# One attention and mixture-of-experts kernel: the dense layers moved between attention steps, blocks fetched by plain transfers, masks in sixteen TensorE tiles

## The chip, the cores and the metric

The kernel runs on one core of one Trainium2 chip. The metric is the device time of one execution in microseconds (us): the median of the runs, beside the lowest and the highest of them. Every count of instructions and every duration below comes from one profiled execution, whose span reaches from the first to the last instruction. PE is TensorE; its loads of the stationary operand are shown on a line of their own.

## The reference, cut to what matters

The first half is attention with a sliding window of 128 keys and a linear distance bias, for 8 batches, 8 heads, 576 positions and head size 64. The second half takes the result as 4608 tokens of 512 numbers. It adds a dense two-layer network to the output of one of eight experts, which is chosen for each token by the largest of eight logits.

```python
scores = np.where(mask, scale * q @ k.T + bias, -1e9)   # 0 <= i - j < 128
attn = softmax(scores)
x = (attn @ v).transpose(0, 2, 1, 3).reshape(4608, 512)
y_dense = np.maximum(x @ w1_dense, 0.0) @ w2_dense
expert_idx = np.argmax(x @ w_gate, axis=1)
# for the tokens of expert e, with the gate probability as a factor:
y_moe[mask] = gate_w[mask, None] * (np.maximum(x[mask] @ w1[e], 0.0) @ w2[e])
return y_dense + y_moe
```

## The kernel before

**Attention.** A *unit* is one batch and four heads, so there are 16 units. A unit has three *steps*: key tiles 0 and 1, tiles 2 and 3, and the half tile 4 (`KP`, L332). That makes 48 steps (`NS`), numbered n. In each step `scores` (L334) lets PE write the masks and biases of four heads into PSUM by matmuls with an identity (L352), adds q.k in 32-row tiles of the array (L363), and ScalarE takes the exponential (L373). VectorE then splits the result into a high and a low bf16 part (`lo`, L392). One step later `attend` (L395) multiplies with v on PE (L426). Two steps later `norm` (L435) divides on VectorE and writes the f32 token row `xrow` (L442). Three steps later `flip` (L451) turns the row by PE and copies it to `xT` on ScalarE (L470). Between these, VectorE turns keys and queries (`turn`, L158) and splits v (`prep_v`, L177), and ScalarE rounds keys (L171) and queries (L168) for PE.

**Order.** PE, ScalarE and VectorE run in the order in which the program is written down, under `tc.manual_schedule` (L594). The order on GpSimd and SyncE is left to the planner. The score tiles and the `ax` tile of the attend matmuls have one PSUM buffer each; everything else in this stage shares the two buffers of `psum_m`.

**Gate and scatter.** After the last step of a batch, `gate_a` to `gate_d` run one step apart. They compute the logits, the chosen expert, its probability and the place (`slot`) of each token in a region of DRAM that belongs to its expert (`xs_dram`). Then GpSimd scatters the rows, 5 indirect transfers a batch (L569). A row is 516 words: 512 numbers, the gate and the token's number. The expert and dense weights, 18 transfers of 512 KB in bf16, are asked for by GpSimd in every second step from n=6 on, each held back by a small copy that waits for a norm (`tick`, L582). Keys, queries and v are loaded by SyncE, one unit ahead.

**Blocks.** After attention, VectorE computes a table of 43 blocks of 128 tokens, each of one expert (L672 to L749). GpSimd gathers a block's rows indirectly (`fetch`, L764) into one of 5 buffers, 4 blocks ahead. `turn_x` casts to bf16 on VectorE (L777), turns by PE and copies out (L784). `layer1` runs the expert's and the dense first layer (L814, L822) with their relus on ScalarE (L830, L831). `turn_h` turns both (L791), VectorE copies out (L797), and `layer2` sums both second layers in PSUM (L849, L857). VectorE copies the sum (L865) and GpSimd scatters it to the output (L866). In the loop the order is

```python
turn_h(j); layer1(j + 1); turn_x(j + 2); layer2(j); fetch(j + AHEAD)
```

## Time and profile before

| what | value |
|---|---|
| median of 3 runs | 508.16 us (503.89 to 510.34) |
| the profiled execution's own time | 514.72 us |
| its span | 513.0 us |
| PE busy | 383.8 us, 75% of the span |
| VectorE busy | 304.0 us, 59% |
| ScalarE busy | 200.3 us, 39% |
| GpSimd busy | 172.5 us, 34% |
| moved by DMA | 66.92 MB, mean 130 GB/s |
| mean granted TensorE clock | 0.882 |

In the profile's slices each digit is the busy share of one fortieth of the span, 12.8 us, in tenths. A row of the groups gives the line, the engine, the operation, the tiles it writes and reads, their shapes and the count; then busy time and the mean duration of one in ns; then the idle time just before and what ended it. A row of the waits names the instruction that waited and the one that released it, and gives the total in us, the number of times, and the longest. The chain goes back from the last instruction to whatever released each one.

### The profile page before, as it was taken

Reading aid. Unit: us, or ns where it says so; the run is one execution under the profiler, and the core shown is the slowest. Engines: PE = TensorE matmul, PEld = TensorE weight load, DVE = VectorE, ACT = ScalarE, POOL = GpSimd, SP = SyncE. Lnnn points to the kernel's source line nnn. Section 1 sums busy time; section 2 is a strip of 40 time slices with the busy share of each in tenths; the row PEclk is TensorE's granted clock in tenths of the full one; section 3 lists DMA queues with packets and bytes.
Section 4 is the critical chain, followed back from the end, with each engine's and each line's share of the span. In section 5 each row is a group of like instructions: output and inputs, shape, how many; then the busy total and the mean of one; then the engine's idle time right before and its main releaser. Section 6 shows DMA issues by size and latency. Waiting matters only on the chain.

```text
span 513.0 us, 10730 instructions
## 1 busy us (share of the span) xinstructions
PE 383.8 (75%) x4143; PEld 240.0 (47%) x4180; DVE 304.0 (59%) x567; ACT 200.3 (39%) x287; POOL 172.5 (34%) x244
## 2 busy tenths in 40 slices
PE   1567877778776787777783039899998999889891
PEld 0345555555554556555562015444454444445450
DVE  5879797775977669867471514444444444444441
ACT  2527656626567156671541003323333222322230
POOL 2000016042151321613113433445545455535531
PEclk9999878876799768997696559999999999999997
DMA  4644979879698697986102220323323333323210
GB/s 135 178 115 118 201 156 246 186 187 210 153 251 175 186 209 166 255 159 202 45 24 90 74 82 33 115 91 98 102 86 111 101 124 103 114 83 119 80 52 0
DMA packets 70912, 66.92 MB, mean 130 GB/s; under 512 B 42446, under 2 KB 61902, under 8 KB 70864
## 3 DMA queue, kind: packets, MB, share of 16 engines
q0 software_dynamic: 19328, 37.91, 29.5%
q1 hardware_dynamic: 51140, 28.01, 20.1%
q8 instruction: 34, 0.56, 0.4%
q10 hardware_dynamic: 396, 0.33, 0.2%
q14 instruction: 14, 0.11, 0.1%
HBM read 58.56 MB, written 20.78 MB: 155 GB/s over the span
## 4 chain that ended last, share of the span: by engine, by line
PE 24%; DMA 13%; DVE 5%; issue 3%; ACT 3%; POOL 1%; another core or an unknown queue 1%; POOLq 0%; DVEq 0%
DMA xr<-xs_dram,row_i 13%; PE y L849 4%; PE y L857 4%; PE hd L822 4%; PE hm L814 4%; ACT hr L831 2%; PE hps L791 2%; DVE xm L777 2%; PE xps L780 2%; PE ax L426 1%; PE lp L486 1%; POOL xs_dram L569 1%; PE lg L498 1%; DMA xs_dram<-xrow,slot 1%
## 5 line engine op out<-in xcount | busy, mean ns | idle before, releaser
L426 PE MATMUL ax<-vf,p 128*128 128x65 bf16 (+1 forms) x576 | 74.9, 215 | 50.6 <-DVE xrow L442 44.5
L373 ACT ACTIVATE p<-sq 128x1024 f32<-128x1024 f32 (+1 forms) x96 | 69.3, 776 | 92.5 <-PE sq L363 70.8
L392 DVE TENSOR_TENSOR plo<-p 128x1024 bf16<-128x1024 f32 (+1 forms) x96 | 82.6, 900 | 28.6 <-ACT p L373 23.1
L426 PEld LDWEIGHTS <-p 128*128 128x128 bf16 (+1 forms) x1152 | 69.9, 113 | 61.2 <-DVE xrow L442 51.2
L830 ACT ACTIVATE hr<-hm,xr 128x512 bf16<-128x512 f32 x43 | 29.5, 687 | 159.7 <-PE hm L814 159.7
L426 PE MATMUL ax<-vf,plo 128*128 128x65 bf16 (+1 forms) x576 | 74.3, 212 | 3.9 <-DVE plo L392 2.8
L866 POOL DMA_INDIRECT out_dram<-yo,tok_i x43 | 44.5, 1034 | 97.1 <-DVE hT L797 88.5
L426 PE MATMUL ax<-vl,p 128*128 128x64 bf16 (+1 forms) x576 | 74.4, 211 | 0.3 <-issue 0.3
L569 POOL DMA_INDIRECT xs_dram<-xrow,slot x40 | 42.7, 1067 | 87.2 <-DVE xrow L561 44.9
L426 PEld LDWEIGHTS <-plo 128*128 128x128 bf16 (+1 forms) x576 | 63.1, 113 | 3.4 <-DVE plo L392 3.3
L865 DVE COPY yo<-y 128x512 f32<-128x512 f32 x43 | 29.7, 692 | 58.0 <-PE y L857 54.1
L352 PE MATMUL sq<-mask,ident_b 128*128 128x512 bf16 (+1 forms) x177 | 46.9, 370 | 15.0 <-DVE mask L235 9.2
L766 POOL DMA_INDIRECT xr<-xs_dram,row_i x43 | 43.8, 1019 | 19.9 <-ACT hr L831 11.3
L822 PE MATMUL hd<-w_all,xT 128*128 128x512 bf16 x172 | 45.0, 385 | 0.0
L849 PE MATMUL y<-w_all,hT 128*128 128x512 bf16 x172 | 44.2, 379 | 0.9 <-DVE hT L797 0.9
L780 PE MATMUL xps<-ident_b,xm 128*128 128x128 bf16 x172 | 17.3, 225 | 36.4 <-DVE xm L777 35.8
L857 PE MATMUL y<-w_all,hT 128*128 x172 | 44.1, 379 | 0.0
L814 PE MATMUL hm<-w_all,xT 128*128 x150 | 40.7, 388 | 3.8 <-DMA xr<-xs_dram,row_i 2.7
L363 PE MATMUL sq<-qT,kT 32*128 32x256 f32 (+2 forms) x640 | 34.7, 330 | 3.4 <-ACT qT L168 3.4
L588 POOL CAST w_all<-xrow 64x1 bf16<-64x1 f32 x18 | 8.1, 447 | 85.4 <-DVE xrow L442 85.1
L784 DVE COPY xT<-xps 128x512 bf16<-128x512 bf16 x43 | 18.3, 425 | 31.0 <-PE xps L780 31.0
L363 PEld LDWEIGHTS sq<-qT,kT 32*128 32x128 f32 x640 | 26.3, 217 | 21.9 <-issue 14.4
(115 smaller groups left out, 570.2 us busy)
## 6 DMA issues: line engine op xcount, KB each, us to landing
kraw<-in_k_dram SPq DMA_DIRECT2D x16, 576.0 KB
vf<-in_v_dram SPq DMA_DIRECT2D x64, 128.0 KB
w_all<-in_moe_w_dram POOLq DMA_DIRECT2D x16, 512.0 KB
qraw<-in_q_dram SPq DMA_DIRECT2D x62, 128.0 KB
vf<-in_v_dram SPq DMA_DIRECT2D x16, 64.0 KB
w_all<-in_moe_w_dense_dram POOLq DMA_DIRECT2D x2, 512.0 KB
qraw<-in_q_dram SPq DMA_DIRECT2D x15, 64.0 KB
xr<-xs_dram,row_i POOLq DMA_INDIRECT x43, 3.4
```

What stands on the lines that cost most here:

```text
L352: nc.tensor.matmul(out=sq[g // 2][:, g % 2, 0:tot], lhsT=ident_b, rhs=rhs, start=True, stop=False,)
L363: nc.tensor.matmul(out=sq[g // 2][:, g % 2, i * wid : i * wid + nq], lhsT=kT[32 * g : 32 * g + 32, c, kj * P : kj * P + P], rhs=qT[32 * g ...
L373: nc.scalar.activation(out=p32[:, :, 0:tot], in_=sq[i][:, :, 0:tot], func=ACT.Exp, scale=SCALE,)
L392: nc.vector.tensor_tensor(out=plo[:, :, 0:tot], in0=p32[:, :, 0:tot], in1=phi[:, :, 0:tot], op=ALU.subtract,)
L426: nc.tensor.matmul(out=ax[:rows, i, o0 : o0 + w], lhsT=lhs, rhs=rhs, start=(n == 1), stop=(n == 3 * len(kl)),)
L569: ins = nc.gpsimd.indirect_dma_start(out=xs_dram[:, :], out_offset=bass.IndirectOffsetOnAxis(ap=slot[:rows, t : t + 1], axis=0), in_=xrow. ...
L766: nc.gpsimd.indirect_dma_start(out=xm_i.bitcast(I32)[:, :], out_offset=None, in_=xs_dram[:, :], in_offset=bass.IndirectOffsetOnAxis(ap=row ...
L814: nc.tensor.matmul(out=hm, lhsT=xT[:, kc, :], rhs=w_all[:, bass.DynSlice(er, 1), 0, kc, :], start=(kc == 0), stop=(kc == 3),)
L822: nc.tensor.matmul(out=hd, lhsT=xT[:, kc, :], rhs=w_all[:, E, 0, kc, :], start=(kc == 0), stop=(kc == 3),)
L849: nc.tensor.matmul(out=y, lhsT=hT[:, c, :], rhs=w_all[:, E, 1, c, :], start=(c == 0), stop=False,)
L857: nc.tensor.matmul(out=y, lhsT=hT[:, 4 + c, :], rhs=w_all[:, bass.DynSlice(er, 1), 1, c, :], start=False, stop=(c == 3),)
L866: nc.gpsimd.indirect_dma_start(out=out[:, :], out_offset=bass.IndirectOffsetOnAxis(ap=tok_i[:, 0:1], axis=0), in_=yo[:, :], in_offset=None ...
```

## The change

- **Dense layers.** They leave the blocks. `dense1` and `dense2` run between the attention steps of the batches, spread over six steps. The first layer holds weights still and moves tokens, and its relu runs on ScalarE. The second layer's result is copied by ScalarE and scattered by GpSimd into a second table, `ys_dram`, with the slots of the tokens.
- **Rounding.** `norm` writes an f32 tile `xf`. ScalarE rounds it to bf16 into `xrow`, whose rows are now 260 words, and `flip` makes two copies, one f32 for the gate and one bf16 for the dense layer.
- **Gate.** `gate_a` runs per unit instead of per batch, and VectorE adds the two parts up (`gate_av`).
- **Routing.** Sixteen blocks are formed from the first six batches in `route_early`, while attention is still running. The other 27 are formed at the end in `late_table`. Every expert's region ends in 128 rows of filling (`late_fill`), so that a block is always 128 rows in a run.
- **Blocks.** They hold the expert's layers alone. A block's x and y rows come by two plain transfers on SyncE at a register's address, seven blocks ahead of the loop's next one, into ten buffers. ScalarE copies the turned h, and VectorE adds the dense result. One block is written down per pass of the same loop from n=50 on, so the last batch's gates and dense layers lie between the first blocks.
- **Masks.** The mask of each head is stored turned by 32 rows per head. Sixteen 32x32 tiles of the array write it instead of four full matmuls per step; each tile has rows and columns of its own.
- **Loads and memory.** v is asked for two units ahead and has three buffers; its first load waits for the first queries. Several buffers shrink. The order on SyncE is now written by hand during attention. The weights are asked for one per 2.33 steps, from n=4 on.

```diff
     NB = NTOK // P + E - 1
-    NSLOT = (E - 1) * NTOK + NB * P
-
-    RW = DM + 4
-    GC = DM
-    TC = DM + 1
+    NQ = 6
+    NE = 16
+    assert (NQ * S - E * (P - 1) + P - 1) // P >= NE
+    NL = NB - NE
+
+    ST = NTOK + P
+    NSLOT = E * ST
+
+    XW = DM // 2
+    RW = XW + 4
+    GC = XW
+    TC = XW + 1
...
@@ -67,8 +75,10 @@
...
+    ys_dram = dram.tile([NSLOT, DM], I32, name="ys_dram")
     w_all = persist.tile([P, E + 1, 2, 4, FF], BF16, name="w_all")
...
+        g = h % 4
+        n = (P, 32, 64, 32)[g]
+        for r in range(0, P, n):
+            t = (r + 32 * g) % P
+            nc.vector.scalar_tensor_tensor(
+                out=mask[t : t + n, h, :],
+                in0=d_f[r : r + n, :],
+                scalar=-slope / SCALE,
+                in1=big[r : r + n, :],
+                op0=ALU.mult,
+                op1=ALU.add,
+            )
...
+    def mask_rest():
         for h in range(4, H):
             mask_head(h)
...
@@ -341,20 +377,24 @@
...
-        for g in range(4):
+
+        for rot, g in [(i, j) for i in range(4) for j in range(4)]:
             h = 4 * hq + g
+            k0 = 32 * rot
+            r0 = (k0 + 32 * g) % P
             if pr == 0:
-                rhs = mask[:, h, 0:PW].unsqueeze(1).to_broadcast([P, 2, PW])
+                rhs = mask[r0 : r0 + 32, h, 0:PW].unsqueeze(1).to_broadcast([32, 2, PW])
             elif pr == 1:
-                rhs = mask[:, h, 0 : 2 * PW]
+                rhs = mask[r0 : r0 + 32, h, 0 : 2 * PW]
             else:
-                rhs = mask[:, h, 2 * PW - TAIL : 2 * PW]
+                rhs = mask[r0 : r0 + 32, h, 2 * PW - TAIL : 2 * PW]
             nc.tensor.matmul(
-                out=sq[g // 2][:, g % 2, 0:tot],
-                lhsT=ident_b,
+                out=sq[g // 2][k0 : k0 + 32, g % 2, 0:tot],
+                lhsT=ident_b[r0 : r0 + 32, r0 : r0 + 32],
                 rhs=rhs,
                 start=True,
                 stop=False,
+                skip_group_check=True,
             )
...
@@ -435,16 +476,21 @@
         def norm():
             if hq == 0 and pr == 0:
                 cur[("xrow", b)] = xrows[b % 2]
-            xrow = cur[("xrow", b)]
+            xrow = cur[("xrow", b)].bitcast(BF16)
+            xf = xpool.tile([P, 2, 256], F32, name="xf", tag="xf")
...
-            xo = xrow[:rows, qis[0] : qis[0] + nt, hq * 256 : hq * 256 + 256]
             nc.vector.tensor_tensor(
-                out=xo.rearrange("p t (h d) -> p t h d", h=4),
+                out=xf[:rows, 0:nt].rearrange("p t (h d) -> p t h d", h=4),
                 in0=ax_v[:rows, 0:nt, :, 0:D],
                 in1=recip[:rows, 0:nt].unsqueeze(3).to_broadcast([rows, nt, 4, D]),
                 op=ALU.mult,
             )
+            nc.scalar.copy(
+                out=xrow[:rows, qis[0] : qis[0] + nt, hq * 256 : hq * 256 + 256],
+                in_=xf[:rows, 0:nt],
+            )
+            cur[("xf", u, pr)] = cur["xf"] = xf
...
@@ -454,54 +500,70 @@
...
         if hq == 0 and pr == 0:
-            cur[("xT", b)] = xpool.tile([P, 4, S], F32, name="xT", tag="xT", bufs=1)
-        xT = cur[("xT", b)]
-        xrow = cur[("xrow", b)]
+            cur[("xTb", b)] = xpool.tile([P, 4, S], BF16, name="xTb", tag="xTb")
+        if pr == 0:
+            cur["xT"] = xpool.tile([P, 2, S], F32, name="xT", tag="xT", bufs=1)
+        xf = cur.pop(("xf", u, pr))
...
+        for dst in (cur["xT"], cur[("xTb", b)][:, 2 * hq : 2 * hq + 2, :]):
+            nc.scalar.copy(
+                out=dst[:, :, q0 : q0 + nt * rows].rearrange(
+                    "p c (t x) -> p t c x", t=nt
+                ),
+                in_=tp[:, 0:nt, :, 0:rows],
+            )
...
-    def gate_a(b):
-        xT = cur[("xT", b)]
-        HF = S // 2
-        for hf in range(2):
-            lp = psum_m.tile([P, 512], F32, name="lp", tag="misc")
-            for ds in range(4):
+    def gate_a(u):
+        lp = psum_m.tile([P, 512], F32, name="lp", tag="misc")
+        for h, (t0, t1) in enumerate(DT):
+            c0, c1 = t0 * P, min(t1 * P, S)
+            for c in range(2):
+                r0 = 64 * h + 32 * c
                 nc.tensor.matmul(
-                    out=lp[32 * ds : 32 * ds + 32, 0:HF],
-                    lhsT=wg_pad[:, ds, :],
-                    rhs=xT[:, ds, hf * HF : (hf + 1) * HF],
+                    out=lp[r0 : r0 + 32, 0 : c1 - c0],
+                    lhsT=wg_pad[:, 2 * (u % HQ) + c, :],
+                    rhs=cur["xT"][:, c, c0:c1],
                     start=True,
                     stop=True,
                 )
...
+    def gate_av(u):
+        lp = gst["lp"]
+        for p0, w in ((64, LW), (0, DT[0][1] * P)):
+            dst = lt[p0 : p0 + 64, 0:w]
+            if u % HQ == 0:
+                nc.vector.tensor_copy(out=dst, in_=lp[p0 : p0 + 64, 0:w])
+            else:
+                nc.vector.tensor_tensor(
+                    out=dst, in0=dst, in1=lp[p0 : p0 + 64, 0:w], op=ALU.add
+                )
...
@@ -572,61 +634,433 @@
                 in_=xrow.bitcast(I32)[:rows, t, :],
                 in_offset=None,
             )
+            apart("x", b, ins)
+        slots[b] = slot
...
+    def after(nm, ins, nb):
+
+        for b, name in writers[nm]:
+            if b < nb:
+                tc.add_manual_dep(
+                    ins.ins,
+                    name,
+                    mybir.DependencyInfo(
+                        mybir.DependencyClass.Sync, mybir.DependencyReason.DATA
+                    ),
+                    reason="rows written",
+                )
...
+    def dense1(b, c, hf):
...
+        hp = psum_m.tile([P, 512], F32, name="hp", tag="misc")
+        for kc in range(4):
+            nc.tensor.matmul(
+                out=hp[:, 0:HF],
+                lhsT=w_all[:, E, 0, kc, c * P : c * P + P],
+                rhs=xTb[:, kc, c0:c1],
+                start=(kc == 0),
+                stop=(kc == 3),
+            )
+        nc.scalar.activation(out=hT[:, c, 0:HF], in_=hp[:, 0:HF], func=ACT.Relu)
+
+    def dense2(b, t):
...
+        yp = psum_m.tile([P, 512], F32, name="yp", tag="misc")
+        for c in range(4):
+            nc.tensor.matmul(
+                out=yp[:rows, :],
+                lhsT=hT[:, c, t0 * P : t0 * P + rows],
+                rhs=w_all[:, E, 1, c, :],
+                start=(c == 0),
+                stop=(c == 3),
+            )
+        yt = xpool.tile([P, DM], F32, name="yt", tag="yt", bufs=4)
+        nc.scalar.copy(out=yt[:rows, :], in_=yp[:rows, :])
+        ins = nc.gpsimd.indirect_dma_start(
+            out=ys_dram[:, :],
+            out_offset=bass.IndirectOffsetOnAxis(
+                ap=slots[b][:rows, t : t + 1], axis=0
+            ),
+            in_=yt.bitcast(I32)[:rows, :],
+            in_offset=None,
+        )
+        apart("y", b, ins)
+
+    def dense_items(b):
+        one = [lambda c=c, h=h: dense1(b, c, h) for h in range(2) for c in range(4)]
+        two = [lambda t=t: dense2(b, t) for t in range(NT)]
+        return [one[0:2], one[2:4], two[0:2], one[4:6], one[6:8], two[2:5]]
...
+    def route_early():
+        fb = whole(0, "a")
+        zero = rt.tile([1, E], F32, name="zero")
+        nc.vector.memset(zero, 0.0)
+        yield
+        er, ro = yield from table(fb, zero, NE, "a")
...
+        for j in range(NE):
+            where[j] = (er[0:1, j : j + 1], st_i[0:1, j : j + 1])
...
+    def late_counts():
+        base_r = rt.tile([1, E], I32, name="base_r")
+        nc.vector.tensor_copy(out=base_r, in_=basee[0:1, :])
+        nb = whole(P - 1, "b")
...
+    def late_table():
+        nb, eb = where["nb"], where["eb"]
+        er, ro = yield from table(nb, eb, NL, "b")
+
+        nc.vector.tensor_tensor(
...
+    def late_fill():
+        base_r = where["base"]
+        for e in range(E):
+            r = nc.values_load(
...
+            ins = nc.sync.dma_start(
+                out=xs_dram[bass.DynSlice(r, P), :], in_=fill_x.bitcast(I32)[:, :]
+            )
+            apart("x", NQ, ins)
+            ins = nc.sync.dma_start(
+                out=ys_dram[bass.DynSlice(r, P), :].rearrange("p (a f) -> p a f", a=2),
+                in_=fill_x.bitcast(I32)[:, 0:XW].unsqueeze(1).to_broadcast([P, 2, XW]),
+            )
+            apart("y", NQ, ins)
...
+    def fetch(j):
+        r = nc.values_load(
...
+        xr = mpool.tile([P, RW], F32, name="xr", tag="xr", bufs=10)
+        yr = mpool.tile([P, DM], F32, name="yr", tag="yr", bufs=10)
+        for nm, t, src in (("x", xr, xs_dram), ("y", yr, ys_dram)):
+            ins = nc.sync.dma_start(
+                out=t.bitcast(I32)[:, :], in_=src[bass.DynSlice(r, P), :]
+            )
+            if j < NE:
+                tc.declare_no_dep(
+                    ins.ins, group=nm + "late", reason="rows of the first NQ batches"
+                )
+                tc.add_to_no_dep_group(nm + "late", ins.ins)
+            after(nm, ins, NQ if j < NE else B)
+        st[("r", j)] = (xr, yr)
...
+    def turn_x(j):
+        xr, _ = st[("r", j)]
+        xps = psum_t.tile([P, 4, P], BF16, name="xps", tag="xps")
+        for kc in range(4):
+            nc.tensor.transpose(
+                out=xps[:, kc, :],
+                in_=xr.bitcast(BF16)[:, kc * P : (kc + 1) * P],
+                identity=ident_b,
+            )
+        xT = mpool.tile([P, 4, P], BF16, name="xTm", tag="xTm")
+        nc.vector.tensor_copy(out=xT, in_=xps)
...
+        hp = psum_h.tile([P, FF], F32, name="hpm", tag="hpm")
+        for kc in range(4):
+            nc.tensor.matmul(
+                out=hp,
+                lhsT=xT[:, kc, :],
+                rhs=w_all[:, bass.DynSlice(er, 1), 0, kc, :],
+                start=(kc == 0),
+                stop=(kc == 3),
+            )
+        hr = mpool.tile([P, FF], BF16, name="hr", tag="hr")
+        nc.scalar.activation(out=hr, in_=hp, func=ACT.Relu, scale=xr[:, GC : GC + 1])
...
+    def turn_h(j):
+        hr, er = st.pop(("g", j))
+        hps = psum_t.tile([P, 4, P], BF16, name="hps", tag="xps")
+        for c in range(4):
+            nc.tensor.transpose(
+                out=hps[:, c, :], in_=hr[:, c * P : (c + 1) * P], identity=ident_b
+            )
+        hT = mpool.tile([P, 4, P], BF16, name="hTm", tag="hTm")
+        nc.scalar.copy(out=hT, in_=hps)
...
+    def layer2(j):
+        hT, er = st.pop(("h", j))
+        xr, yr = st.pop(("r", j))
+        y = psum_y.tile([P, DM], F32, name="y", tag="y")
+        for c in range(4):
+            nc.tensor.matmul(
+                out=y,
+                lhsT=hT[:, c, :],
+                rhs=w_all[:, bass.DynSlice(er, 1), 1, c, :],
+                start=(c == 0),
+                stop=(c == 3),
+            )
+        yo = mpool.tile([P, DM], F32, name="yo", tag="yo", bufs=4)
+        nc.vector.tensor_tensor(out=yo, in0=y, in1=yr, op=ALU.add)
...
+    AHEAD = 7
...
+    def block(j):
+        if j == 0:
+            turn_x(0)
+            layer1(0)
+            turn_x(1)
+        turn_h(j)
+        if j + 1 < NB:
+            layer1(j + 1)
+        if j + 2 < NB:
+            turn_x(j + 2)
+        layer2(j)
+        if j + AHEAD + 1 < NB:
+            fetch(j + AHEAD + 1)
...
     with tc.manual_schedule(engines={ENG.PE, ENG.Activation, ENG.DVE}):
+        mask_consts()
         turn(0, "k")
         round_qk(0, "k")
-        mask_consts()
+        mask_head(0)
+        mask_head(1)
         turn(0, "q")
         round_qk(0, "q")
+        mask_head(2)
+        mask_head(3)
...
+        loads = ExitStack()
+        loads.enter_context(tc.manual_schedule(engines={ENG.SP}))
+        while jm < NB:
+            if n == NS:
+                loads.close()
+            if n > NS + 1:
+                block(jm)
+                jm += 1
+            if 0 <= n - 3 < NS:
+                flip(*steps[n - 3])
+                u2, pr2 = steps[n - 3]
+                b2 = u2 // HQ
+                if pr2 == 2:
+                    items.setdefault(n, []).append(lambda u=u2: gate_a(u))
+                    gates.setdefault(n + 1, []).append(lambda u=u2: gate_av(u))
+                if u2 % HQ == HQ - 1 and pr2 == 2:
...
+                    for i, fs in enumerate(dense_items(b2)):
+                        items.setdefault(n + 2 + i, []).extend(fs)
+                    if b2 == NQ - 1:
+                        gen = route_early()
...
+            for f in gates.pop(n, []):
+                f()
             if n == 0:
-                more_constants()
                 prep_v(0)
+            todo = items.pop(n, [])
+            for f in todo[:1]:
+                f()
             if 0 <= n - 1 < NS:
                 norms[n - 1] = attend(*steps[n - 1])
+            for f in todo[1:]:
+                f()
...
                 else:
+                    if u + 2 < NU:
+                        load_v(u + 2)
```

## The prediction

> **What bounds the kernel now.** I read three views in this order: the page's slices, to find the stages; the sums by stretch, to see how full each engine is in each; then the waits and the chain in order of time, to see which wait ends last.
>
> ```profile
> PE   1567877778776787777783039899998999889891
> ...
> DVE  5879797775977669867471514444444444444441
> ACT  2527656626567156671541003323333222322230
> ...
> PEclk9999878876799768997696559999999999999997
> DMA  4644979879698697986102220323323333323210
> ```
>
> Three stages show. Up to slice 22 (some 277 us) is attention: PE and VectorE share the load, ScalarE is half idle, DMA is nearly full. Slices 23 and 24 are a hole. The rest is 43 blocks, with PE alone busy.
>
> ```profile
> 200.00:225.00 25.00, 20.63 (x314) 14.95 (x316) 20.86 (x39) 14.58 (x23) 9.49 (x10) 0.86 0.90 209
> ...
> 275.00:300.00 25.00, 1.95 (x14) 1.74 (x13) 9.19 (x37) 0.24 (x1) 10.00 (x13) 0.50 0.18 60
> ...
> 400.00:450.00 50.00, 46.73 (x305) 24.04 (x310) 24.13 (x46) 14.12 (x22) 24.73 (x33) 1.00 0.35 111
> ```
>
> The columns are PE, weight loads, VectorE, ScalarE, GpSimd, granted clock, DMA share, GB/s. In attention no engine is full (PE and VectorE 21 of 25 us). The waits say why:
>
> ```profile
> ACT p L373 <- PE sq L363: 70.8, 30, 7.7
> ...
> PE ax L426 <- DVE xrow L442: 44.5, 26, 5.5
> ...
> DVE plo L392 <- ACT p L373: 23.1, 12, 4.3
> ```
>
> Exp waits for scores, the attend matmuls (L426) for VectorE's norm, VectorE's split (L392) for exp: a ring of three engines. Unit 4's key transpose (late in step n=9) starts at 60.1 us and the last mask matmuls (n=47) at 259.4: about 5.3 us a step. The hole is the last batch's gates, scatters, routing table and first gather: PE's last gate matmul ends at 276.6, the first block matmul starts at 304.1. The blocks:
>
> ```profile
> 406.81 0.86 PE y L849 x4
> 407.67 0.86 PE y L857 x4
> 408.98 0.86 PE hm L814 x4
> 409.84 0.88 PE hd L822 x4
> 410.74 0.61 ACT hr L831
> 411.38 3.27 DMA xr<-xs_dram,row_i
> ```
>
> From 304 to 503 us is 43 x 4.63 us. A gather can start only when a row buffer is free (after L831), and its 3.3 us end on the path every other block; PE's own work is about 4.2 us of the 4.63.
>
> **The blocks afterwards.** The dense half goes, and so do the x casts, as rows arrive as bf16. PE per block: 4+4 transposes (x8 take 0.45 in the chain) and two groups of four matmuls (0.86 each): 0.45 + 1.72 = 2.17 us. Beside it ScalarE has a relu (0.69, L830) and the copy of the turned h, priced by L831 (0.60): 1.29. VectorE has xT (0.43, L784) and an add, priced by L442's same shape (0.69): 1.12. GpSimd has one scatter of 1.03. The relu has 1.09 us of PE work as cover (4 transposes and layer 2 of the block before), so neither evacuation ends on the path. DMA: x 128 x 1040 B, y 128 x 2048 B, out 128 x 2048 B, 657 KB; at the 400:450 rate (111 GB/s at share 0.35, 317 GB/s full) 2.07 us. Gathers leave GpSimd for SP, issued eight blocks, some 18 us, before use, so the 3.3 us are covered; two direct issues and a register load per block on SP are bounded below by 0.7 (0.34 is the row of a lone key load) and above by 2 us (each queued behind others, as in attention, 1 us): under the block either way. So PE at 2.17, DMA close behind. I take 2.33, PE at its 400:450 share of 0.935: 43 x 2.33 = 100 us, where it was 199. Ends 2.17 (93 us) and 2.9 (126, DMA at attention's rate, 207 GB/s at 0.92).
>
> **The hole.** Blocks 0 to 15 use only batches 0 to 5 and a table made in steps 42 to 46; so block 0 waits for one fetch after attention frees its memory, 3 us (a gather takes 3.3). Batch 7's gates and dense part now sit between blocks 0 and 7: PE 8.1 dense + 2.5 gates = 11 us. VectorE's late gates and table (some 37 small operations of 0.2, L509's row) lie in blocks 2 to 6, beside matmuls; I count 3 of their 7 us. GpSimd has 10 + 8 scatters of 1.05 = 19 us in these 8 steps of about 3.5 us, so they fit, and fetch 16, queued on SP behind the fills and behind every batch-7 scatter, has 7 blocks of cover. If that cover fails, all later fetches stand behind it: up to 10 us.
>
> **Attention afterwards.** Per batch (6 steps):
> - *PE.* Before, 198 us in 275, 24.8 a batch at the granted clock of about 0.85; some 22.6 from warm rows. Dense: layer 1 streams 16 x 256 + 16 x 320 columns, 3.9 us at L849's warm rate (0.86 per 4 x 512); layer 2, 20 matmuls, 4.3. Masks save about 0.8. That is 5.4 us a step at the old clock, 5.0 warm.
> - *ScalarE.* Rows:
>
> ```profile
> L373 ACT ACTIVATE p<-sq 128x1024 f32<-128x1024 f32 x64 | 62.1, 1021 | 89.9 <-PE sq L363 68.2 <-remote 14.2 <-issue 7.5
> ...
> L831 ACT ACTIVATE hr<-hd 128x512 bf16<-128x512 f32 x43 | 25.7, 597 | 6.3 <-PE hd L822 1.2
> ...
> L470 ACT COPY xT<-tp 128x512 f32<-128x512 f32 x32 | 19.0, 593 | 6.2 <-remote 3.2 <-PE tp L464 3.0
> ```
>
>   Before: 145 us, 18.1 a batch. Added: the second flip copy and the rounding of xf, each 4 x 0.59 + 2 x 0.29 = 2.9; eight relus at 0.40 (the 288-wide copy L493); five copies of y at 0.60; gone: two L493. 2.9 + 2.9 + 3.2 + 3.0 - 0.8 = 11.2. 29.3 a batch, 4.9 a step; it was 3.0.
> - *VectorE.* 3.9 a step, plus two adds or copies per unit, 0.8: 4.2. The early table, 5 us once, goes into its gaps.
> - *DMA.* Before, about 13.3 us per engine and unit. ys adds 288 rows per unit, xs rows halve: +1.8 - 0.7, 14.4 in a longer unit, so share 0.8, not above today's. v is asked for two units ahead, which removes most of VectorE's 24 us of DMA waits, some 0.3 us a step. GpSimd gains 40 scatters, 42 us over 240, off the path. Weights come one per 2.33 steps instead of 2, the last at step 44, before any block needs it.
>
> So three engines need 4.2, 4.9 and 5.0 to 5.4 us. The ring, over two steps: split 2.3, norm 0.9, attend 1.5, dense items 1.3, flip 0.6, scores 1.1, first exp 1.0, some 0.6 between engines: 9.3; then ScalarE's key rounding (2.2, L171) ahead of the next flip copies and exp, of which PE work covers half: about 11.5. I take 5.9 a step. Ends: 5.2 (ScalarE nearly gapless) and 6.9 (5.4 at today's PE share, 0.78). 40 steps (10 to 49): 236 us.
>
> *A rule against this.* The Trainium skill, "TensorEngine Tiling (Array Packing)", PSUM Bottleneck, says tiling speeds TensorE but not PSUM evacuation, and wants ScalarE and VectorE both used; here every new evacuation is ScalarE's. By the rows that is 6.2 us of the 11.2 a batch; were it split evenly, ScalarE would need 4.4, VectorE 4.7, and by the rule I would say 5.5 a step, 16 us less. The change doesn't split, so the rows stand.
>
> *Masks.* Four full matmuls take 0.95 us to the first q.k matmul (129.69 to 130.64). The same page (Key Properties) says a tiling-mode switch drains the array, and the change adds one per step; "TensorE: Matmul & The Clock Gate", Measured speedup, gives 660 ns for a 16-tile, 512-column pack. By the pages: 0.95 - 0.66 - a drain. The trace has a drain: 0.42 us of idle weight load before L363, of which 0.21 is the last mask streaming, so 0.2; gain 0.1. By rows: L363's 16 tiles start within 0.35 us, so 0.35 + 0.21 + 0.2 = 0.76, gain 0.2. In 16 narrow steps the sixteen starts cost 0.15 more than today. I take 0.2 x 32 - 0.15 x 16 = 4 us of PE work over all, the drain included (ends -5 and +10); as PE has gaps, 0 on the end.
>
> **Start.** Pieces for three quarters of the heads make 22 mask instructions of 0.62 instead of 8: 14 more, 9 us of VectorE. Six of them sit before the first scores, where q, no longer sharing with v (held behind it by a GpSimd copy), should come earlier. I count +5 (ends 1 and 9): n=10, at about 61 before, starts at 66.
>
> **Sum, on the profiled execution** (span 513.0, own time 514.7): 66 + 236 + 3 + 11 + 3 + 100 = 419; then the tail (503.0 to 513.0, unchanged) 10 and 1.7 around the span: 431. That execution is 1.3% above the median shown (508.16), so against the median 431 x 508.16/514.72 = 425 us.
>
> **Rivals.**
> - *ScalarE and PE overlap almost fully*, 5.2 a step: 28 less, 398. For: no DMA waits. Against: two bufs of psum_m tie PE's items to ScalarE's order. 0.16.
> - *DMA bounds the blocks* at 2.9 us: 26 more, 450. For: 1040-byte rows, two tables, the fills. Against: rows of 2 KB kept 317 GB/s. 0.14.
> - *Early fetches aren't early* (the first blocks wait for the last batch after all): the hole of 28 us returns, 452. 0.06.
> - *The clock drops*, on the other side. PE needs 5.0 us warm per step; at 5.9 a step a granted clock under 0.85 makes PE the ring, and at 0.62 (8.1 us) the result is 2% slower. At 0.58: 8.6 us, 40 x 2.7 = 108 more, 532. For: 0.67 at 100:125 and 0.63 at 242:253. Against: those dips follow idle PE (17.1 of 25 and 7.0 of 11 us busy); dense matmuls fill it. 0.05; near no change 0.05.
> - Main case: 0.54, alone 408 to 446.
>
> Range: lower end short of the first rival, 396; the upper takes in DMA and 6.7 us steps, 468. A measurement of this kernel tells 2% from no change; faster by more 0.90, within 0.05, slower 0.05.
>
> **What would show it.** Right: step spacing of the exps near 5.9 with ScalarE above 80% in attention; no hole; y groups 2.2 to 2.5 us apart at clock 1.0 and DMA share above 0.8. Wrong: steps at 5.2 or 7; a gap before block 16; DMA landing just ahead of the transposes of x; PE's clock under 0.8.

## The result, and the profile after

The changed kernel takes 421.51 us (median of 4 runs, 417.0 to 426.11), the kernel before 509.25 in the same comparison: a ratio of 0.824 (95% interval 0.815 to 0.833). The prediction was 425. The profiled execution took 424.43 us with a span of 422.7; it and one other ran slower than the rest, at a lower mean clock (0.926 and 0.938 against 0.941 to 0.971), and the ratio leaves these two out. One thing has to be known for all that follows: the changed kernel took 419 to 422 us in two of the comparisons (one on chip 1, the other's chip isn't known) and 465 to 466 in two others (chips 15 and 10), while the kernel before stayed between 504 and 516 in all four. No chip is known to have been used in two comparisons, so what belongs to the chip and what to the hour can't be told apart. So kernels are compared only within one group of runs on one chip; each group has its own execution of the changed kernel.

The slices of the changed kernel, now 10.6 us each (busy tenths, granted clock, DMA share):

```profile
PE   1445989499899797898797989887789899999990
...
DVE  7899898679879778889786799861336344444440
ACT  3244785679789787799786799854436555555550
...
PEclk9986586789999998999997999998989999999997
DMA  4454677597979786979886955629938999888720
```

The hole is gone: PE has no slice below 7 from the ninth to the last but one. ScalarE, which showed 1 to 7 in attention before, now shows mostly 7 to 9 beside PE and VectorE. DMA is close to full in attention and again in the blocks. The last attention step's exps lie in slice 27.

The blocks, first by windows (busy PE, weight loads, VectorE, ScalarE, GpSimd, then clock, DMA share, GB/s), then by the chain in order of time (start, length, what):

```profile
350.00:375.00 25.00, 24.36 (x167) 13.30 (x170) 11.85 (x21) 13.32 (x21) 10.01 (x11) 1.00 0.87 278
375.00:400.00 25.00, 24.42 (x170) 13.42 (x172) 11.67 (x22) 13.42 (x21) 10.64 (x11) 1.00 0.86 273
```

```profile
347.78 0.22 PE hps L940 x4
348.00 0.04 issue
348.03 1.02 PE hpm L925 x4
349.06 0.22 PE xps L904 x4
349.28 0.86 PE y L952 x4
```

PE holds 97% of each window. One turn of the chain is 0.22 + 0.04 + 1.02 + 0.22 + 0.86 = 2.36 us, and it contains nothing but PE. The one step that isn't as predicted is `hpm` (the expert's first layer): 1.02 instead of 0.86.

In attention (70 to 280 us) the waits name a different last arrival than before, and so does the chain:

```profile
DVE qs L162 <- DMA qraw<-in_q_dram: 12.5, 6, 4.0
...
DVE plo L433 <- ACT p L414: 6.5, 12, 1.1
```

```profile
190.13 1.39 DVE qs L162
...
193.32 1.10 SPq L140
194.47 12.26 DMA qraw<-in_q_dram
206.92 1.39 DVE qs L162
208.32 0.56 SPq L140
208.93 0.54 SPq L140
209.52 0.53 SPq L140
210.09 0.53 SPq L140
210.66 12.43 DMA qraw<-in_q_dram
```

VectorE's split waits 6.5 us for exp, where it waited 23.1. What the chain runs through is the queries: four issues on SP once the single raw buffer is free, 12 us of transfer, the transpose that frees the buffer, and again. From one transpose at 190.13 to the next at 206.92 it is 16.8 us, and a unit of three steps at 5.48 us takes 16.4.

### The profile page after: what moved, and what is told of

It is laid out like the page before. It is cut to its first block, busy times and chain, and to the rows that moved or that the text cites. A ratio compares the mean times of both kernels' runs of the same rounds, so it can differ in the third digit from the quotient of the medians.

```text
span 422.7 us, 12201 instructions
## 1 busy us (share of the span) xinstructions
PE 345.6 (82%) x4628; PEld 220.3 (52%) x4656; DVE 288.9 (68%) x566; ACT 276.5 (65%) x471; POOL 167.8 (40%) x197
## 4 chain that ended last, share of the span: by engine, by line
PE 25%; DMA 22%; DVE 20%; issue 11%; ACT 6%; POOL 6%; SPq 5%; another core or an unknown queue 1%; POOLq 1%; ACTq 0%; DVEq 0%
DMA qraw<-in_q_dram 18%; DVE plo L433 6%; POOL out_dram L961 6%; PE ax L467 5%; SPq L140 4%; DVE qs L162 4%; PE hpm L925 4%; PE yp L692 3%; PE y L952 3%; PE hp L677 3%; DMA vf<-in_v_dram 2%; DVE xf L483 2%; DVE mask L258 2%; ACT p L414 2%; PE lg L557 1%
## 5 line engine op out<-in xcount | busy, mean ns | idle before, releaser
L467 PE MATMUL ax<-vf,p 128*128 128x65 bf16 (+1 forms) x576 | 70.0, 209 | 19.2 <-DVE xf L483 18.9
L467 PEld LDWEIGHTS <-p 128*128 128x128 bf16 (+1 forms) x1152 | 67.1, 110 | 30.6 <-DVE xf L483 23.9
L961 POOL DMA_INDIRECT out_dram<-yo,xr x43 | 42.6, 991 | 69.0 <-DVE yo L960 46.5
L467 PE MATMUL ax<-vl,p 128*128 128x64 bf16 (+1 forms) x576 | 69.5, 206 | 0.0
L467 PE MATMUL ax<-vf,plo 128*128 128x65 bf16 (+1 forms) x576 | 69.4, 207 | 0.0
L701 POOL DMA_INDIRECT ys_dram<-yt,slot x40 | 47.1, 1178 | 37.4 <-ACT yt L700 27.1
L467 PEld LDWEIGHTS <-plo 128*128 128x128 bf16 (+1 forms) x576 | 60.8, 109 | 0.0
L677 PE MATMUL hp<-xTb,w_all 128*128 128x256 bf16 (+1 forms) x256 | 43.4, 295 | 13.8 <-ACT hTd L684 7.0
L925 PE MATMUL hpm<-w_all,xTm 128*128 x163 | 44.3, 387 | 5.2 <-issue 2.5
L933 ACT ACTIVATE hr<-hpm,xr 128x512 bf16<-128x512 f32 x43 | 29.6, 687 | 23.4 <-PE hpm L925 18.2
L952 PE MATMUL y<-w_all,hTm 128*128 x166 | 43.7, 383 | 1.1 <-ACT hTm L944 0.8
L960 DVE TENSOR_TENSOR yo<-y,yr 128x512 f32<-128x512 f32 x43 | 29.7, 691 | 21.3 <-PE y L952 20.6
L684 ACT ACTIVATE hTd<-hp 128x256 bf16<-128x256 f32 (+1 forms) x64 | 25.6, 411 | 27.1 <-PE hp L677 26.7
L692 PE MATMUL yp<-w_all,hTd 128*128 128x512 bf16 (+1 forms) x147 | 40.1, 381 | 3.8 <-ACT yt L700 1.7
L172 ACT CAST kT<-ks 128x1152 fp32r<-128x1152 f32 x16 | 35.3, 2209 | 2.3 <-DVE ks L162 2.3
L517 ACT COPY xT<-tp 128x512 f32<-128x512 f32 (+1 forms) x48 | 23.1, 481 | 19.9 <-PE tp L510 19.8
```

Source lines behind the costliest of these rows:

```text
L172: nc.scalar.copy(out=d[:, :, 0:S].rearrange("p c (x r) -> p c x r", r=R), in_=s.rearrange("p c (r x) -> p c x r", r=R),)
L467: nc.tensor.matmul(out=ax[:rows, i, o0 : o0 + w], lhsT=lhs, rhs=rhs, start=(n == 1), stop=(n == 3 * len(kl)),)
L677: nc.tensor.matmul(out=hp[:, 0:HF], lhsT=w_all[:, E, 0, kc, c * P : c * P + P], rhs=xTb[:, kc, c0:c1], start=(kc == 0), stop=(kc == 3),)
L692: nc.tensor.matmul(out=yp[:rows, :], lhsT=hT[:, c, t0 * P : t0 * P + rows], rhs=w_all[:, E, 1, c, :], start=(c == 0), stop=(c == 3),)
L701: ins = nc.gpsimd.indirect_dma_start(out=ys_dram[:, :], out_offset=bass.IndirectOffsetOnAxis(ap=slots[b][:rows, t : t + 1], axis=0), in_=y ...
L925: nc.tensor.matmul(out=hp, lhsT=xT[:, kc, :], rhs=w_all[:, bass.DynSlice(er, 1), 0, kc, :], start=(kc == 0), stop=(kc == 3),)
```

## The experiments

Two measures are used beside the medians, both from the traces: a *step* is the mean distance of the first exps from n=10 to n=47, and a *block* the mean distance of the `yo` additions from block 11 to 42. The first four runs shared a chip (15), the next four another (1), the last four a third (10). `before` is the kernel before in the same group.

### First group

`again`: the changed kernel unchanged.

> The changed kernel once more, beside the three kernels of this call, as their base. Expected as before: about 421 us, 0.82 of the kernel before, steps 10 to 47 at 5.5 us each, a unit of three steps every 16.4 us.

Measured 465.28 us (459.24 to 469.61; before 516.01; ratio 0.904, 0.891 to 0.916). Step 6.19 instead of 5.48, block 2.47 instead of 2.36. The instructions on every engine have the same order as in the first trace, so this is no other schedule; more on it under the third group.

`masks_full`: the sixteen tiles undone.

```diff
-        n = (P, 32, 64, 32)[g]
+        n = P
...
-            t = (r + 32 * g) % P
+            t = r
...
-        for rot, g in [(i, j) for i in range(4) for j in range(4)]:
+        for g in range(4):
...
```

> The masks part alone is undone: four full matmuls with the identity per step, and one mask instruction per head. By the prediction's sum the sixteen tiles save 4 us of PE work in all and nothing on the end, and the pieces of the masks cost 9 us of VectorE at the start, of which 5 end on the path: so undoing it makes the kernel 3 to 7 us faster (n=10 near 66 instead of 72 us) with the steps unchanged at 5.5. Rival, PE's order sets the steps: each wide step grows by the 0.4 us that the mask group takes longer (0.65 against 1.04 us), 32 x 0.4 = 13 us, less the 6 won at the start: 7 us slower. Rival, transfers set the steps: steps unchanged, 5 us faster.

Measured 453.39 us (448.16 to 460.1; ratio 0.887, 0.879 to 0.895), 11.9 less than `again`. The first exp of n=10 comes at 66.6 us instead of 71.0, which is the start as predicted: VectorE's mask instructions take 5.4 us in all instead of 15.0, and the very first exp comes at 16.6 instead of 18.8. A step took 6.00 instead of 6.19, another 7 us over 37 steps. The mask matmuls themselves did what they should in the changed kernel: 24.4 us of PE in all, against 41.8 with full masks (groups of `again3` and `masks_full2`, the same two kernels in the third group of runs):

```profile
L391 PE MATMUL sq<-mask,ident_b 32*32 32x512 bf16 (+1 forms) x768 | 24.4, 364 | 15.4 <-DVE mask L258 13.3 <-ACT p L414 1.7
```

```profile
L389 PE MATMUL sq<-mask,ident_b 128*128 128x512 bf16 (+1 forms) x192 | 41.8, 337 | 14.2 <-DVE mask L258 12.5 <-ACT p L412 1.6
```

So the tiles make PE less busy, and yet the kernel with them is the slower one. It would be wrong to read from this that the masks are off the path. A *wide* step is one with two key tiles, two of the three in a unit. In a wide step the first q.k matmul follows the first mask matmul by 0.37 us with tiles and by 0.96 with full masks (medians), and where nothing else is late the distance of two exps that ends with a wide step grows with it, from 3.78 to 4.25 us and from 4.68 to 5.18. What is shorter with full masks is the start, and those steps in which the engines are held; the third group shows them.

`yt_vector`: the copy of the dense result out of PSUM moved from ScalarE to VectorE.

```diff
-        nc.scalar.copy(out=yt[:rows, :], in_=yp[:rows, :])
+        nc.vector.tensor_copy(out=yt[:rows, :], in_=yp[:rows, :])
```

> Only the copy of the dense result out of PSUM (L700, 40 times 0.6 us) moves from ScalarE to VectorE: the evacuations are split between the two engines, as the skill's rule wants. If ScalarE's load sets the steps (the prediction's reading), ScalarE goes from 4.9 to 4.4 us a step and the kernel becomes up to 16 us faster. If the round trip of the queries or the transfers set the steps, the result is within 3 us of the changed kernel. If VectorE's place in the ring counts (split, norm, attend), it is 5 to 15 us slower.

Measured 507.47 us (504.57 to 510.75; ratio 0.991, 0.986 to 0.996): 42 us more than `again`, a step of 7.44. Forty copies of 0.6 us are 24 us of work, so more than the copies is lost. It is the third expected reading, at three times its size. The waits of this kernel between 100 and 300 us:

```profile
DVE yt L700 <- PE yp L692: 31.5, 22, 3.2
PEld L591 <- issue: 17.2, 5, 3.5
...
PE pc L591 <- DVE oh L579: 16.5, 5, 3.3
```

VectorE now stands 31.5 us in its fixed order waiting for dense matmuls, and the gate operations, splits and norms behind each copy stand with it; PE in turn waits 16.5 us for one of these gate operations (`oh`). PE was busy for 75 to 78% of this stretch, at a granted clock of 0.78 to 0.80. The rule weighed in the prediction (the Trainium skill, "TensorEngine Tiling (Array Packing)", PSUM Bottleneck: evacuate with both engines) would have made this the faster kernel by up to 16 us. The measurement decides against it here.

`q_two`: two raw query buffers, asked for two units ahead (one `yt` buffer and a table of filling are given up for the memory).

```diff
-        t = ld.tile([P, R, 2, 32], F32, name="qraw", tag="qraw", bufs=1)
+        t = ld.tile([P, R, 2, 32], F32, name="qraw", tag="qraw", bufs=2)
...
+        load_q(2, nc.sync)
...
-                        if u + 1 + 1 < NU:
-                            load_q(u + 1 + 1, nc.sync)
+                        if u + 3 < NU:
+                            load_q(u + 3, nc.sync)
```

> The queries get a second buffer and are asked for two units ahead (the dense result has three buffers instead of four for room, and the filling is made when it is needed). In the changed kernel a unit is turn of the queries 1.4 us, five issues 3 to 6 us, and about 12.5 us until the last one lands, 16.4 us in all, and the chain of waits goes through that landing. Theory A, the round trip of the single buffer sets the unit: the waits of VectorE for queries (14 us) vanish and a unit takes 15 us or less, 15 to 20 us off the end. Theory B, the DMA engines' throughput sets it (share 0.84 in the middle of attention): the wait moves to another load, the unit stays at 16.4 us, within 4 us of the changed kernel. Theory C, the engines' ring sets it: also within 4 us, and no load is waited for.

Measured 465.91 us (462.83 to 468.77; ratio 0.913, 0.906 to 0.920), the same as `again`. On this chip VectorE waits for queries only 4.5 us in all in `again`, against 14.0 in the first execution, so the loop read from the first chain could not be tested here.

### Second group

`again2`, the changed kernel unchanged:

> The changed kernel once more, unchanged, as the base of the three runs beside it. In the two executions looked at so far its steps from 10 to 47 took 5.48 us each (421 us in all) and 6.19 us (465 us), with the same order of instructions on every engine. If the difference belongs to the chip that it ran on, this run lies anywhere between 415 and 475 us and only the step and the first blocks move with it; the blocks from 11 to 42 stay at 2.3 to 2.5 us.

Measured 419.18 us (417.92 to 424.17; before 503.95; ratio 0.834, 0.829 to 0.840), step 5.48, block 2.36: the first execution over again.

`static_expert`: a constant in place of the number that PE loads for each block. The weights that a block takes are then not those of its rows.

```diff
-        er = nc.values_load(
-            where[j][0],
-            engines=[ENG.PE],
...
+        er = None
...
-                rhs=w_all[:, bass.DynSlice(er, 1), 0, kc, :],
+                rhs=w_all[:, j % E, 0, kc, :],
...
-                rhs=w_all[:, bass.DynSlice(er, 1), 1, c, :],
+                rhs=w_all[:, j % E, 1, c, :],
```

> The expert of each block is a constant (block number modulo eight) instead of a number loaded into PE's registers; the weights that a block takes are then not those of its rows, all else is as in the changed kernel. Theory A: PE paces the blocks, and what stood over the predicted 2.17 us a block is PE's stop for that register; then blocks 11 to 42 take 2.15 to 2.20 us and the whole is 7 to 9 us faster than the changed kernel beside it. Rival B: row fetches and write-backs pace them (about 0.87 of the DMA engines' time was busy in that stretch), and PE only seems full because its waits are short; then the blocks stay within 0.05 us of the changed kernel's.

Measured 412.61 us (410.82 to 413.73; ratio 0.819, 0.816 to 0.823), 6.6 us less than `again2`, just short of the 7 to 9 expected. From block 16 to 40 a block takes 2.17 us instead of 2.37. PE's group of the first layer in `static_expert` between 345 and 400 us, and then the register load in `again2` (least, median and greatest ns):

```profile
L919 PE MATMUL hpm<-w_all,xTm 128*128 128x512 bf16 x96 | 25.1, 379 | 0.2
```

```profile
L914 PEldq TENSOR_LOAD <-erb x27: 297/303/342, 341.4 to 403.0; - x27
```

The load takes 0.30 us and 0.2 of it shows. Without it the block is the sum of PE's matmuls and transposes, at a DMA share of 0.91 (350 to 375 us): PE paces the blocks, and the transfers hadn't quite reached their limit. (Over all blocks the mean fell only to 2.25, because block 13 came 2.1 us late in this trace.)

`one_expert`: every block takes the first expert, and only its weights and the dense ones are loaded, 4 of 18 transfers.

```diff
-        nc.vector.tensor_copy(out=er, in_=s3[:, 0, :])
+        nc.vector.tensor_scalar_mul(out=er, in0=s3[:, 0, :], scalar1=0.0)
...
-            while wnext < 2 * (E + 1) and n < NS and wnext <= 18 * (n - 4) / 42:
+            while wnext < 4 and n < NS and wnext <= 18 * (n - 4) / 42:
```

> All blocks take the first expert's weights, and of the nine experts' weights only the dense one's and the first expert's are loaded (4 of 18 loads); the products of the other experts are left out. What it tells: whether the attention steps are held by DMA throughput. Theory A (the ring of PE, VectorE and ScalarE sets a step, the transfers lie beside it): steps 10 to 47 within 0.15 us of the changed kernel's beside it, the whole within 8 us. Rival B (q, k and v come late because the weight loads, the row scatters and the early row fetches share the DMA engines, whose busy share was 0.78 to 0.88 in the attention stage): steps 0.3 to 0.6 us shorter, the whole 12 to 25 us faster. The blocks should not change either way, since all weights are in place before them.

Measured 407.85 us (406.3 to 409.53; ratio 0.810, 0.807 to 0.814), 11.3 less than `again2`; step 5.17 instead of 5.48, blocks unchanged. Windows of attention, `again2` first, then `one_expert`:

```profile
160.00:200.00 40.00, 34.82 (x586) 23.13 (x586) 31.67 (x55) 33.31 (x60) 18.70 (x20) 0.96 0.86 207
```

```profile
160.00:200.00 40.00, 37.20 (x658) 24.97 (x654) 33.89 (x60) 35.35 (x62) 15.18 (x14) 1.00 0.65 193
```

The DMA share falls from 0.86 to 0.65 and all three engines get denser; VectorE's waits for queries fall from 12.2 us in `again2` to 1.4 (and 2.8 put down to v). Six steps now repeat with hardly a change: 3.7, 4.7, 5.2, 3.8, 6.8, 6.0 us, 5.03 on average. In `again2` each place in this series of six reaches the same value at its shortest (n from 11 to 45), and single steps are longer. So these values are the ring of the engines, and what stood above it was late data. (GpSimd loses 14 weight issues too; that these lie beside the ring is argued from their place in it, not tested.) Rival B holds, at the lower end of its size for the step and just under it for the whole.

`late_blocks`: blocks only after the last batch's work is issued.

```diff
-            if n > NS + 1:
+            if n > NS + 10:
```

> The blocks begin only when the last batch's steps are all issued, not two steps after the last attention step; the work is the same. Theory A: PE's work of the last batch (about 11 us) and that of the first blocks fill each other's gaps; apart they cost 8 to 15 us more. Rival B: the two get in each other's way (the mixed stretch took some 12 us more than the sum of the parts in the first execution, with waits on VectorE's routing chain standing between blocks); apart, the batch's steps run at their own pace and the blocks at 2.36 us from the first, and the whole comes out the same within 5 us or up to 8 us faster.

Measured 420.51 us (417.66 to 423.44; ratio 0.835, 0.830 to 0.840), 1.3 more than `again2`. From the exp of n=47 to the first `yo` it is 37.0 us instead of 16.5, and from there to the last 98.7 instead of 117.7. So the last batch's gates and dense part cost 20.5 us on their own and 19.0 mixed with blocks. Mixing hides next to nothing.

### Third group

`again3`, the changed kernel unchanged:

> The changed kernel unchanged, as the base of the three runs beside it: 415 to 425 us with steps of about 5.5 us, or, if its chip is like the one on which it took 465 us, about 460 with steps of about 6.2.

Measured 466.25 us (464.06 to 470.73; before 514.98; ratio 0.905, 0.899 to 0.911), step 6.40: like the first group. Here is a look at what happens about once in two units. Windows of one to two microseconds, and the chain through them:

```profile
239.00:240.00 1.00, 0.50 (x11) 0.29 (x8) 0.00 (x0) 0.00 (x0) 0.69 (x2) 1.00 1.18 271
240.00:241.00 1.00, 0.46 (x4) 0.18 (x4) 0.00 (x0) 0.00 (x0) 0.52 (x1) 1.00 1.14 316
241.00:242.00 1.00, 0.59 (x3) 0.32 (x4) 0.00 (x0) 0.56 (x1) 0.00 (x0) 1.00 1.10 323
...
244.00:246.00 2.00, 1.57 (x20) 0.86 (x20) 1.90 (x4) 1.28 (x3) 0.24 (x1) 0.50 0.15 57
```

```profile
239.24 0.33 PE ax L467 x5
239.57 0.42 issue
239.99 1.48 PE ax L467 x2
```

From 240 us on PE lets three or four attend matmuls a microsecond through, and VectorE and ScalarE stand nearly still, though the profile shows nothing that PE waits for and the DMA engines are at their fullest. Then the clock is at half for 6.8 us. The Trainium skill ("TensorE: Matmul & The Clock Gate", HAM oscillation — how this bites in real kernels) describes such a cycle: a wait longer than the activity window, and the work after it at half rate. This trace agrees in the half clock that follows; what differs is that PE let single matmuls through for some 3.5 us instead of standing still, and that the profile shows no wait for data. In `again2` the same place has a DMA share of 1.1 to 1.2 as well, and PE runs on. The weight loads of the attend matmuls (L467) waited 18.0 us for "issue" in the stretch from 60 to 320 us of `again3`, and 5.5 in `again2`.

ScalarE is held as well. These are the first exps of step n=28 in `again3` and in `one_expert`, with the same instructions around them; in brackets the idle time before:

```profile
190.45 1.02 ACT L414 ACTIVATE p<-sq 128x1024 f32<-128x1024 f32 x1 [0.80 <-PE pc L599]
```

```profile
168.79 1.02 ACT L414 ACTIVATE p<-sq 128x1024 f32<-128x1024 f32 x1
```

The last q.k matmul had ended 0.91 us before the first of them and 0.04 us before the second, and `pc`, which is named as the releaser, had ended 0.65 us before the first. The holds stand at the same places in every batch. This is the distance of the first exps from step n to n+1 by n modulo six, the six steps of a batch (medians, n from 10 to 46, in us):

| n modulo six | 0 | 1 | 2 | 3 | 4 | 5 |
|---|---|---|---|---|---|---|
| `one_expert` | 4.68 | 5.21 | 3.75 | 6.75 | 6.03 | 3.70 |
| `again3` | 7.03 | 5.53 | 3.78 | 7.62 | 6.02 | 7.55 |

`again`, on the other of the two slower chips, has 7.64 and 7.62 at the places 3 and 5. So the 45 us more aren't a slower ring: the places 2 and 4 take what they take elsewhere, and most of the rest is added at fixed places of the program. On the same chip as `again`, `yt_vector`, with another order on ScalarE and VectorE, has 6.75 at place 3. Why the engines are held there was not found.

`masks_full2`, the edit of `masks_full`:

> The sixteen mask tiles undone once more (four full matmuls a step, masks not turned), beside another execution of the base. Theory A: where transfers hold the attention steps (about 0.84 of the DMA engines' time busy, steps 5.48 us where the steps without late data take 5.03), PE's work doesn't set the step; then the 0.5 us that full masks add to PE change no step, and only the earlier start is left: 3 to 6 us faster, all of it before step 10. Rival B: the tiles' cost is in the ring of every step, as the earlier comparison read (0.19 us a step): 10 to 14 us faster. Rival C, the change's own reason: less PE work pays, and full masks are 4 to 10 us slower.

Measured 454.93 us (452.3 to 455.9; ratio 0.883, 0.876 to 0.889), 11.3 less than `again3`: the size of rival B for the second time, but not by its reading. The start is 5.6 us earlier at n=10, a step 6.15 instead of 6.40. By place the six distances are 5.18, 6.24, 4.24, 7.53, 6.02 and 6.59: place 2, which isn't held, is longer than with tiles (4.24 against 3.78), and the held places 0, 3 and 5 are shorter. (Place 1 is longer here, 6.24 against 5.53, and shorter in the first pair.) The "issue" wait of the attend weight loads falls from 18.0 to 5.7 us. Full masks have 1152 fewer instructions on PE, and the profile's queue of instructions has 33 packets instead of 38. That the engines wait for instructions would fit this, and one packet lands just as PE goes on after the trickle above (244.41 and 244.42 us). But of the 47 idle stretches of PE over 0.4 us between 60 and 320 us of `again3` only four end within 0.3 us of a packet's landing, so this isn't the bulk of it.

Whether full masks gain anything on a chip without these holds wasn't tried, and the undisturbed steps speak against it. With 0.46 to 0.50 us more in each of the 24 wide steps up to n=47 they would lose some 12 us there and win about 5 at the start: by this estimate, from `again2`, `one_expert` and the two full-mask runs, 7 us slower, unless waits for queries hide a part.

`masks_q2`: full masks and two query buffers.

> Full masks, and beside them two buffers for the raw queries, each asked for two units ahead instead of one (one buffer fewer for the dense layer's results and a second use of the xf buffers pay for the memory). Theory A: the queries come late because their single buffer is asked for only once it is free, and the transfer then takes 10 to 12 us among the others; asked for a unit earlier they are there, steps 10 to 47 fall to between 5.1 and 5.3 us, and the whole is 7 to 14 us faster than with full masks alone. Rival B: the transfers are late by throughput, not by when they are asked for; then k, v or the scatters are late in their place and the whole stays within 4 us of the run with full masks alone.

Measured 451.06 us (446.94 to 452.22; ratio 0.878, 0.872 to 0.884), 3.9 less than `masks_full2`, with overlapping 95% intervals of the ratio. The step falls from 6.15 to 5.90, but n=10 starts 4.0 us later; the third queries, which are now asked for ahead of other early loads, may be why. Inconclusive by itself. It is still the fastest full kernel of its group: 15 us under the changed kernel and 64 under the one before.

`ahead3`: rows fetched three ahead.

```diff
-    AHEAD = 7
+    AHEAD = 3
```

> Rows of the blocks are fetched three ahead of the loop's next block instead of seven; nothing else. A block takes 2.36 us, so three ahead still leave about 7 us for a transfer. Theory A: the lead isn't what the blocks need, PE paces them; the blocks 11 to 42 stay at 2.3 to 2.4 us, and the whole within 4 us of the changed kernel's. Rival B: with 386 KB asked for and 256 KB written in every block the transfers take over 7 us each, rows come late, and the blocks take 2.6 us or more: 8 us slower or worse.

Measured 468.47 us (462.53 to 471.46; ratio 0.903, 0.894 to 0.912), not distinguishable from `again3` (464.06 to 470.73); blocks from 16 to 40 at 2.36 us in both. A lead of three is enough. The kernel before fetched four ahead and its blocks did wait for rows, so what freed them isn't the number seven: the plain transfers, the larger number of buffers, or both. No run separates these.

## Why the prediction was right, point by point

The total came out 7 us under the working on the profiled execution (431 against 424.43). That it came so near is luck, as two large errors cancel, one of 25 us and one of 14:

| term of the sum | predicted, us | measured, us |
|---|---|---|
| start of n=10 (first of its mask matmuls) | 66 | 72.4 |
| 40 steps and the first fetch | 239 | 213.8 (first block transpose at 286.2) |
| batch 7, late table and 43 blocks | 114 | 128.3 (last `yo` ends at 414.5) |
| tail and around the span | 11.7 | 9.9 |
| sum | 431 | 424.4 |

- **Start.** Five late was predicted, on a start of "about 61" that was read 4 us too early: the mask matmuls of n=10 began at 65.2 in the kernel before. With that the addition was 7 in this execution (4 to 5 in `again`, `again2` and `again3`), and the two full-mask runs give 4.4 and 5.6 to the mask pieces.
- **Steps.** The step that failed is the ring: 11.5 us over two steps, from which 5.9 was taken. `one_expert` shows it at 10.1 (5.03 a step). A slip in the sum is most of it: the pieces make 9.3, and half of the key rounding's 2.2 makes 10.4, but 11.5 counts it whole, although PE's work was said to cover half. With 10.4 the step would have been 5.2, and the 0.8 us by which the measured ring exceeds the pieces is about that half. ScalarE needs 4.5 us a step (83% of 5.48), not 4.9, and PE 4.8, not 5.0 to 5.4. The reading that DMA waits would mostly go was half right: VectorE's fell from 24 to about 15 us. What is left of them, queries instead of v, goes with the other transfers in `one_expert`, and 0.31 us a step with it. So the first rival (5.2 a step) had the better step, and transfers, at a share of 0.84 to 0.87 between 100 and 240 us where 0.8 was accepted as harmless, are the reason that it wasn't reached. The 5.48 lies between the 5.9 named as right and the 5.2 named as wrong; ScalarE is above 80%, as named.
- **No hole.** Right. The first fetch is issued at 283.1, in the middle of the last batch's work, and the first transpose follows 3.1 us later. The rival of late early fetches is out.
- **Batch 7 among the blocks.** The second failed step: 11 us of PE work and 3 for VectorE make 14; `late_blocks` gives 19.0 mixed, 20.5 apart. The 11 us rest on PE's rows at full clock. Between 275 and 350 us PE was busy 64.8 of 75 us, against 73 in steady blocks, at a clock of 0.93 in two of the three windows. Those 8 us of idle time and the slower clock account for most of the difference: the likely reason, not tested, is the chain of gate, count and table operations on VectorE, which stands between matmuls whether blocks are there or not. The sum also had no term for filling the loop: from the first transpose to the end of the first addition it is 8.2 us, 5.8 more than a block.
- **Blocks.** PE as the bound, right: 2.17 is what `static_expert` measures. The 0.16 to 2.33 was taken as a general loss of 6.5%; it is one instruction, the load of the expert's number, at 0.20. The rival of DMA at 2.9 is out. Its need in the prediction, 2.07 us a block, fits the measured share (0.86 of 2.36 is 2.03), so DMA would be next.
- **Masks.** PE's saving was put at 0.2 us a wide step, or 0.1 by the pages it cites, with a loss in the narrow ones, and at nothing on the end. Measured it is 0.59 to the first q.k matmul (0.37 against 0.96), with no loss in narrow steps (0.18 against 0.22): the 0.37 is little more than the 0.35 expected for sixteen starts, and the 0.21 and 0.2 added for the last tile and a drain don't show. The first q.k tiles start while the last mask tiles still stream. In undisturbed steps 0.5 of it shows in the ring. That the tiles would cost nothing there did not hold on the two slower chips: 11 to 12 us with the start.
- **Clock.** 0.926 granted in the first execution. A rival feared less than 0.85 in attention; from 100 us on it was 0.91 or more, before that 0.83. In the two slower comparisons the profiled executions had 0.927 (`again`) and 0.902 (`again3`), so the mean clock alone can't make their 45 us more.

## What to carry to other kernels

When an engine takes over work in a ring of three, look at what else stands behind that work in its fixed order: the same 40 copies cost 42 us more on VectorE, which closes the ring, than on ScalarE. Work laid among other work hides only if it leaves gaps to be filled: the last batch's gates and dense part cost 19.0 us among the blocks and 20.5 apart from them. And once the engines are dense, look at which load comes late and what it shares the DMA engines with: here the queries were on time once 14 other loads were gone. Whether a second buffer for them does the same was not settled. Last, measure a step where nothing is late before judging a change in it: the total alone called the mask tiles a loss, while in undisturbed steps they save 0.5 us.

## What the runs showed of the hardware

The same program, instruction for instruction, took 419 and 422 us in two comparisons and 465 and 466 in two others, on chips 15 and 10, with ranges of 6 to 10 us within each, while the kernel before spread over 504 to 516. A gain that is measured in one comparison can be little more than half as large in another (ratios 0.824 and 0.834 against 0.904 and 0.905). A load of one number into a PE register took 0.30 us, of which 0.20 could not be hidden by a full queue of matmuls, 8% of a block. Sixteen 32x32 mask tiles let the next q.k group start after 0.37 us, where four full matmuls took 0.96. And in two of the comparisons PE and ScalarE were held at the same places of every batch, though the profile shows nothing unfinished that they waited for; the steps there were longer by 0.9 and 3.9 us.
